# Transposing q on VectorE instead of TensorE in a fused attention and gated feed-forward kernel

## The chip, the cores and the metric

The kernel runs on one core of a Trainium2 chip. A core has five engines, each with its own instruction stream in order: TensorE (PE, matrix products; PEld in the profile is its weight load), VectorE (DVE), ScalarE (ACT), GpSimd (POOL) and SyncE (SP, which here only starts transfers). Sixteen DMA engines move data between the HBM and the on-chip SBUF. The metric is the device time of one execution in microseconds (us). The kernel before took 934.76 us, the median of three runs (934.28 to 935.01). The profiled execution took 934.53 us, and its instructions span 932.8 us; the TensorE clock was granted at 0.999 of full speed.

## The reference

```
kv  = einsum('bhsd,bhse->bhde', k, v)          # 8 x 8 x 576 x 64
out = einsum('bhsd,bhde->bhse', q, kv)
out = out / sqrt(mean(out*out, -1) + 1e-6) * g_norm
x   = out as (8*576, 8*64)                      # 4608 tokens of 512
h   = x @ w_in                                  # 512 -> 2048
g   = h * erf(softplus(h))
result = g @ w_out                              # 2048 -> 512
```

There is no softmax: each head multiplies q by the small 64 x 64 matrix k^T v, normalizes by the root of the mean square of its 64 outputs, and the 512 outputs of a token go through a gated feed-forward block. w_in and w_out arrive as 64-bit floats and are converted on the chip.

## The kernel before, in words

**Groups.** The 4608 tokens are worked in nine groups T of 512. Groups 0 to 7 are the first 512 rows of each of the eight batch entries; the remaining 64 rows of each entry are gathered in `x_last` and make group 8. The eight heads of a group are worked in four pairs p. So there are 32 pairs (T, p), and the pair after (T, p) is called `then` in the code.

**Attention of a pair.** TensorE needs q with the channels on partitions. For T = 0 the function `products` (L426) transposes q with TensorE; this stays. For the 28 pairs of T = 1 to 7, `turn_products` (L293) makes 16 products of 64 x 64 blocks of q with an identity matrix, and in every second pair 4 more for the last 64 rows (`q_last`); `turned` (L339) copies them from PSUM to the SBUF tile `qT` on ACT, and `tails_kept` (L352) copies the last rows on DVE. `kv_products` (L321) makes the 20 products of k^T v, and `kv_kept` (L361) stores the sum in `bd_kv`. `visit` (L459) multiplies qT by bd_kv into the PSUM tile `at`, ACT squares the result, and `mean` (L524) averages the squares over the channels of a head by a product with the matrix `mean_w`. `norm` (L558) finishes on DVE.

**Where turning and k^T v are done.** For T = 1 and 2 and for the pair (3, 0), `prepare` (L376) does turning and k^T v of a pair as a block of its own before the pair's visit (nine blocks). From T = 3 on (`fused`), the visit of a pair does both for the next pair, with the turned blocks in a pair of PSUM banks of their own (19 visits).

**Two kinds of mean.** In groups 2 to 7 (`halves`), `halve` (L517) splits the squares on DVE into a rounded upper part and a rest, both of type fp32r, and the mean is two products on these. In groups 0, 1 and 8 the mean is one plain fp32 product.

**Feed-forward.** Groups 0 and 1 run step by step (32 steps n, 16 to a group) with weights held in SBUF. While group 1 is worked the weights are cut into three parts each and stored to DRAM (`w_upper`, `w_lower`, L688 to L717). From group 2 on, h and the result are computed from such parts as sums of fp32r products (L677), in batches of four of the 16 column blocks; a batch is four products pairs for h and four for the result. The loop at L1014 runs over the 28 batches of groups 2 to 8. Each batch fetches the weight parts of the next one: four tiles w_in_parts and four w_out_parts of 768 KB each (`load_parts`, L807), from pools of 4 and 7 tiles. The attention of group T + 1 is cut into pieces and laid into the batches of group T, one pair to a batch; `places` (L1030) says after which product each piece comes. Everywhere the order of instructions is the order of the Python program, by hand (`manual_schedule`).

**Transfers.** Nearly all go out from SP, in program order. `load_pair` (L122) fetches q, k and v of a pair, two pairs ahead, into pools of two buffers. q of a pair is one transfer of 256 KB in runs of 256 bytes; k and v for T > 0 are each one transfer with 115 rows on the partition side and one of a single row; `load_last` (L147) fetches the last rows of q, four transfers to a group. In the compiled program SP's transfers use eight completion counters in turn, and each transfer waits for the one eight places before it to have landed.

Of the kernel before, what the change touches and what calls it, by code (L numbers as in the profile page):

```python
# [56 lines left out]
SHIFT = 4096.0  # L57


@with_exitstack  # L60
def kernel(
# [54 lines left out]
    q_last = const.tile([P, 2, 2, D], FP32, name="q_last")  # L116
# [5 lines left out]
    def load_pair(i):  # L122
        T, p = divmod(i, NP)
        if T >= B:
            return
        pool = early if i in (2, 3) else kvp
        side = nc.scalar if i < 3 else nc.sync
        t = q_sb[T, p] = pool.tile([P, J, 2, D], FP32, name="q_sb", tag="q")
        nc.sync.dma_start(
            out=t, in_=q[T, 2 * p : 2 * p + 2, 0:G, :].rearrange("h (p j) d -> p j h d", j=J)  # L130
        )
        for name, got, src in (("k", k_sb, k), ("v", v_sb, v)):
            C = chunks(T)
            rows, rest = divmod(S, C)
            assert rest < 2
            t = got[T, p] = pool.tile([rows + rest, 2, C, D], FP32, name=f"{name}_sb", tag=name)
            heads = src[T, 2 * p : 2 * p + 2]
            side.dma_start(
                out=t[:rows].rearrange("r h c d -> r h (c d)"),
                in_=heads[:, : S - rest].rearrange("h (r c) d -> r h (c d)", c=C),  # L140
            )
            if rest:
                side.dma_start(
                    out=t[rows:, :, 0], in_=heads[:, S - rest :].rearrange("h r d -> r h d")
                )

    def load_last(T, p):  # L147
        if T < B:
            nc.sync.dma_start(
                out=q_last[p % 2 * R : p % 2 * R + R, p // 2],  # L150
                in_=q[T, 2 * p : 2 * p + 2, G:S, :].rearrange("h r d -> r h d"),
            )
# [6 lines left out]
    for i in range(NP - 1):  # L159
        load_pair(i)  # L160
        if i == 0:
            load_last(0, 0)
            load_last(0, 1)
# [7 lines left out]
    ident = const.tile([P, P], FP32, name="ident")  # L171
    make_identity(nc, ident)
    mean_w = const.tile([P, P], FP32R, name="mean_w")
    mean_f = early.tile([P, P], FP32, name="mean_f", bufs=1)
# [118 lines left out]
    def turn_products(T, p, ps):  # L293


        qs = q_sb.pop((T, p))
        for j in range(J):
            for r in range(2):
                for i in range(2):
                    out_ = ps[r][rows_of[i if r == 0 else 1 - i], 0 : 2 * P]  # L300
                    yield partial(
                        nc.tensor.matmul,
                        out_.rearrange("d (t j) -> d j t", j=J)[:, j],
                        lhsT=qs[rows_of[r], j, i],
                        rhs=ident[rows_of[r], rows_of[r]],
                        start=True,
                        stop=True,
                    )
        if p % 2 == 0:
            for r in range(2):  # L310
                for i in range(2):
                    yield partial(
                        nc.tensor.matmul,
                        ps[r][rows_of[i], 2 * P : 2 * P + R],
                        lhsT=q_last[rows_of[r], p // 2, i],
                        rhs=ident[rows_of[r], rows_of[r]],
                        start=True,
                        stop=True,
                    )

    def kv_products(T, p, at, crossed):  # L321
# [4 lines left out]
        for c in range(C):  # L326
            for r in range(2):
                rows = (slice(0, D), slice(D, S // C + (c < S % C)))[r]
                for i in range(2):
                    yield partial(  # L330
                        nc.tensor.matmul,
                        at[rows_of[i], r ^ i if crossed else r, kv_cols],
# [5 lines left out]

    def turned(T, p, ps):  # L339

        qT = attp.tile([P, G], FP32, name="qT", tag="qT")
        if isinstance(ps, tuple):
            for a in range(2):
                nc.scalar.copy(halves_of(qT)[:, a], ps[a][:, 0 : 2 * P])
        else:
            nc.scalar.copy(halves_of(qT), ps[:, :, 0 : 2 * P])
        if p == NP - 2:
            for i in range(NP):
                load_last(T + 1, i)
        return qT  # L350

    def tails_kept(T, p, ps, qT):  # L352

        if p % 2 == 0:
            tails[T] = attp.tile([P, 2, R], FP32, name="qT_last", tag="t")
            for a in range(2):
                t = ps[a] if isinstance(ps, tuple) else ps[:, a]
                nc.vector.tensor_copy(out=tails[T][:, a], in_=t[:, 2 * P : 2 * P + R])
        ready[T, p] = qT, tails[T][:, p % 2]
# [16 lines left out]
    def prepare(T, p):  # L376

        at = at_tile()
        for product_ in turn_products(T, p, (at[:, 0], at[:, 1])):
            product_()  # L380
        for product_ in kv_products(T, p, at, crossed=False):
            product_()  # L382
        qT = turned(T, p, at)

        def keep():
            tails_kept(T, p, at, qT)
            kv_kept(T, p, at)

        kept.append(keep)
# [3 lines left out]
    def keep_prepared():  # L393
        kept.pop()()

    def attention(T, p, pools=None, in_parts=False):
# [3 lines left out]
        halves = FIRST <= T < B  # L400
        quad = 0 < T < B
        fused = FIRST < T < B
# [17 lines left out]
        def square_tile(name):  # L420
# [3 lines left out]
            return attp.tile([P, G], FP32, name=name, tag="sq_lo" if fused else "qT")  # L424

        def products():  # L426
# [17 lines left out]
            if p == NP - 2:  # L444
                for i in range(NP):
                    load_last(T + 1, i)
# [3 lines left out]
            if p % 2 == 0:  # L450
                tails[T] = attp.tile([P, P], FP32, name="qT_last", tag="t")
# [7 lines left out]
        def visit():  # L459


            qT, tail = ready.pop((T, p))
            at = st["at"] = at_tile()
            x = halves_of(qT)
            for a, i, o in ((0, 0, 0), (0, 1, 1), (1, 0, 1), (1, 1, 0)):
                nc.tensor.matmul(  # L466
                    at[rows_of[o], a, 0 : 2 * P],
                    lhsT=bd[rows_of[i], a * D : a * D + D],
# [4 lines left out]
            for s in rows_of:  # L473
                nc.tensor.matmul(
                    at[s, 0, 2 * P : 2 * P + R], lhsT=bd[s, 0:D], rhs=tail[s], start=True, stop=True
                )
            st["o"] = at[:, :, 0 : 2 * P]
            st["next"] = fused and then[0] < B
            if st["next"]:
                ps = pair_of_banks("q0_ps", "q1_ps")  # L480
                kvs = list(kv_products(*then, at, crossed=True))
                turns = list(turn_products(*then, ps))
                while kvs or turns:
                    for some in (turns, kvs):
                        for product_ in some[:4]:
                            product_()  # L486
                        del some[:4]
            if fused:
                st["sq"] = x_new.tile([P, G], FP32, name="sq", tag="x")
            else:  # L490
                st["sq"] = qT
            nc.scalar.activation(two(st["sq"]), st["o"], AF.Square)
            if st["next"]:
                st["turned"] = ps, turned(*then, ps)

        def keep_tail():
            nc.vector.tensor_copy(
                out=x_last[:, p, T * R : T * R + R], in_=st["at"][:, 0, 2 * P : 2 * P + R]
            )
            if st.get("next"):  # L500
                tails_kept(*then, *st.pop("turned"))
# [94 lines left out]
        if T == 0:  # L596
            return products, apply, halve, mean, norm
        if T == B:
            return lambda: None, square, lambda: None, mean, norm, split

        prepare_ = partial(prepare, T, p)
        if fused:
            first_ = (prepare_, keep_prepared) if (T, p) == (FIRST + 1, 0) else ()
            pieces = (first_, (visit, halve, keep_tail), (loads,))
        elif halves:
            pieces = ((prepare_,), (visit,), (halve, keep_tail, loads))
        else:
            pieces = ((prepare_, loads), (visit,), (keep_tail,))
        after = (split_upper, split_lower) if in_parts else (split,)
        return (*(partial(chain, *group) for group in pieces), mean, norm, *after)  # L610
# [163 lines left out]
    load_last(0, 2)  # L774
    load_last(0, 3)
# [11 lines left out]
    for i in range(NP + 3):  # L787
# [3 lines left out]
        if i == 1:  # L791
            for _ in range(RAW - 2):
                w_next("load")
            load_pair(NP)
            load_pair(NP + 1)
# [4 lines left out]
    w_late.append(True)  # L800
    first_batch, batches = FIRST * NB, NG * NB
# [17 lines left out]
    def pieces_of(T):  # L819


        steps = [([], [], []) for _ in range(FC)]
        for p in range(NP):
# [5 lines left out]
            steps[f + 2][0].append(halve)  # L829
# [34 lines left out]
    for n in range(FIRST * FC + 1):  # L864
# [10 lines left out]
        if T < FIRST:  # L875
# [5 lines left out]
            while kept:  # L881
                keep_prepared()
            for key in list(w_new)[:2]:
# [37 lines left out]
        if T < FIRST:  # L921
# [21 lines left out]
            if n == 0:  # L943
                w_next("split")
            for piece in steps[f][1]:
# [68 lines left out]
    for m in range(first_batch, batches + 1):  # L1014
        T, b = divmod(m, NB)
        todo = []
        turn = b == NB - 1 and T + 1 < B
        if T + 1 < NG:
            todo = list(attention(T + 1, b, in_parts=turn))
# [11 lines left out]
        if T + 1 == B:  # L1031
            places = (0, 0, 0, 5, 6, 7)
            if b == NB - 1:


                places, todo[3] = (0, 0, 0, 4, 6, 7), partial(todo[3], table=False)
                todo[5] = partial(chain, todo[5], softplus_table)
        elif turn:


            places, todo[3] = (0, 2, 3, 4, 5, 5, 6), partial(todo[3], table=False)
# [10 lines left out]
        to_last = m == B * NB - 1  # L1052
# [33 lines left out]
        if m < batches:  # L1086
            for i in range(1 if turn else 2):
# [5 lines left out]
        for j in range(J):  # L1093
# [12 lines left out]
            else:  # L1106
                due_halves = range(2) if j == (2 if to_last or turn else 1) else ()
            if to_last or turn:
                pieces(BATCH + 1 + j)
            if turn and j == 0:  # L1110
# [43 lines left out]
```

## Time and profile before

| | us | what it is |
|---|---|---|
| run, median of 3 | 934.76 | 934.28 to 935.01 |
| span of the profiled execution | 932.8 | first to last instruction |
| PE busy | 916.4 | 98% of the span, 5998 products |
| DVE busy | 728.5 | 78% |
| ACT busy | 603.4 | 65% |
| products of the turning in visits (L486, q_ps) | 20.6 and 3.1 | 608 on q_sb, 72 on q_last |
| products of the turning in blocks (L380) | 6.3 and 1.5 | 288 on q_sb, 40 on q_last |
| ACT copies of turned q (L344, L346) | 12.1 and 5.3 | 38 of 128x256, 9 of 128x512 |

Busy time of a group of instructions is the time in which at least one of them ran; products are pipelined and several 64 x 64 products run at once, so these times overlap with each other and with other rows. An fp32 product shows as two records. What a block of products costs is better read from the times at which it and the next block start.

### The profile page before, as it was taken

The numbers are of one execution on the slowest core, as the hardware profiler recorded it, in microseconds if no ns is written. First come the engines' busy times: TensorE is split into PE (matmuls) and PEld (weight loads), VectorE is DVE, ScalarE is ACT, GpSimd is POOL, SyncE is SP. The second block draws the span as 40 slices with busy tenths as digits, with TensorE's granted clock in tenths as the row PEclk, the third lists the DMA queues.
The fourth block names the chain that finished last, engine by engine and source line by source line (L and its number), as shares of the span: only waits on it lengthen the run. The fifth ranks groups of instructions, "written<-read, shape, count | busy, mean of one in ns | idle before, by whom it ended". The sixth has DMA issues, their size and how long they took to land.

```text
span 932.8 us, 15394 instructions
## 1 busy us (share of the span) xinstructions
PE 916.4 (98%) x5998; PEld 684.5 (73%) x5998; DVE 728.5 (78%) x1074; ACT 603.4 (65%) x830; POOL 2.4 (0%) x10
## 2 busy tenths in 40 slices
PE   6999999999999999999999999999999999999998
PEld 4444445665588888888888888888888888888886
DVE  2888848888578888888878888888888887886777
ACT  3877666777666666666656666666666766665552
POOL 1000000000000000000000000000000000000000
PEclk9999999999999999999999999999999999999999
DMA  9866406888799998899889989988897778778871
GB/s 257 288 207 211 144 1 224 312 344 316 225 352 320 334 332 283 293 338 316 286 295 321 317 297 308 324 311 299 282 345 269 270 265 333 286 282 312 330 270 53
DMA packets 108272, 260.01 MB, mean 279 GB/s; under 512 B 43992, under 2 KB 66856, under 8 KB 108200
## 3 DMA queue, kind: packets, MB, share of 16 engines
q1 hardware_dynamic: 106488, 256.73, 78.2%
q10 hardware_dynamic: 1648, 2.29, 0.8%
q8 instruction: 48, 0.79, 0.3%
q14 instruction: 24, 0.20, 0.1%
q0 software_dynamic: 64, 0.00, 0.0%
HBM read 224.40 MB, written 34.60 MB: 278 GB/s over the span
## 4 chain that ended last, share of the span: by engine, by line
PE 94%; ACT 2%; DVE 2%; DMA 1%; issue 0%; DVEq 0%; ACTq 0%
PE n_ps L677 47%; PE m_ps L677 23%; PE o_ps L733 9%; PE h_ps L914 6%; PE at_ps L466 2%; PE at_ps L486 1%; PE q_ps L486 1%; PE at_ps L380 1%; PE at_ps L537 1%; PE at_ps L538 1%; PE ms_ps L543 1%; PE at_ps L382 1%; DMA v_sb<-in_v_dram 1%; DMA q_sb<-in_q_dram 1%; DVE w_new L645 0%
## 5 line engine op out<-in xcount | busy, mean ns | idle before, releaser
L677 PE MATMUL n_ps<-w_out_parts,g_forms 128*128 128x512 f32 x928 | 231.9, 392 | 0.0
L677 PE MATMUL n_ps<-x_forms,w_in_parts 128*128 128x512 f32 x896 | 224.2, 392 | 0.0
L677 PEld LDWEIGHTS n_ps<-w_out_parts,g_forms 128*128 128x128 f32 x928 | 172.8, 188 | 37.2 <-issue 1.9
L677 PEld LDWEIGHTS n_ps<-x_forms,w_in_parts 128*128 128x128 f32 x896 | 166.5, 188 | 35.3
L1082 ACT ACTIVATE s<-h 128x512 f32<-128x512 f32 x112 | 70.8, 632 | 176.1 <-DVE h L655 176.0
L655 DVE TENSOR_TENSOR h<-m_ps,h 128x512 f32<-128x512 f32 x116 | 80.0, 689 | 80.6 <-ACT h L1067 55.7
L677 PE MATMUL m_ps<-w_out_parts,g_forms 128*128 128x512 f32 (+1 forms) x468 | 124.3, 388 | 0.0
L677 PE MATMUL m_ps<-x_forms,w_in_parts 128*128 128x512 f32 x448 | 119.8, 389 | 0.0
L733 PE MATMUL o_ps<-w_out_sb,h_sb 128*128 128x512 f32 x224 | 101.7, 597 | 0.2 <-DVE h_sb L862 0.2
L677 PEld LDWEIGHTS m_ps<-w_out_parts,g_forms 128*128 128x128 f32 x468 | 87.4, 188 | 18.5
L677 PEld LDWEIGHTS m_ps<-x_forms,w_in_parts 128*128 128x128 f32 x448 | 84.1, 188 | 17.6
L655 DVE TENSOR_TENSOR e<-m_ps,e 128x512 f32<-128x512 f32 (+1 forms) x117 | 80.4, 687 | 14.8 <-PE m_ps L677 3.6
L1067 ACT ACTIVATE h<-n_ps 128x512 f32<-128x512 f32 x112 | 66.1, 591 | 19.0 <-PE n_ps L677 18.9
L733 PEld LDWEIGHTS o_ps<-w_out_sb,h_sb 128*128 128x128 f32 x224 | 41.4, 189 | 44.6 <-issue 41.9
L621 DVE SCALAR_TENSOR_TENSOR g_forms<-g_forms 128x1024 fp32r<-128x1024 f32 x58 | 71.1, 1225 | 2.0
L618 DVE TENSOR_TENSOR g_forms<-h,g_forms 128x1024 fp32r<-128x1024 f32 x58 | 70.6, 1217 | 0.1
L615 ACT ACTIVATE g_forms<-h 128x1024 fp32r<-128x1024 f32 x58 | 58.4, 1050 | 15.1 <-PE m_ps L677 11.1
L1114 DVE TENSOR_TENSOR h<-h,s 128x1024 f32<-128x1024 f32 x56 | 65.9, 1218 | 0.0
L914 PE MATMUL h_ps<-xT,w_in_sb 128*128 128x512 f32 x144 | 64.8, 596 | 0.2 <-DVE w_in_sb L245 0.2
L650 DVE SCALAR_TENSOR_TENSOR e<-n_ps,e 128x512 f32<-128x512 f32 x88 | 60.2, 684 | 3.9 <-PE n_ps L677 3.9
L108 ACT ACT_TABLE_LOAD x44 | 56.5, 1283 | 0.7
L1088 ACT ACTIVATE s<-s 128x1024 f32<-128x1024 f32 x51 | 51.5, 1054 | 0.3
(129 smaller groups left out, 1028.9 us busy)
## 6 DMA issues: line engine op xcount, KB each, us to landing
w_out_parts<-w_out SPq DMA_DIRECT2D x116, 768.0 KB
w_in_parts<-w_in SPq DMA_DIRECT2D x112, 768.0 KB
w_in<-w_new SPq DMA_DIRECT2D x16, 768.0 KB
q_sb<-in_q_dram SPq DMA_DIRECT2D x32, 256.0 KB
w_raw<-in_moe_w_in_dram SPq DMA_DIRECT2D x16, 512.0 KB
w_raw<-in_moe_w_out_dram SPq DMA_DIRECT2D x8, 1024.0 KB
out_dram<-e SPq DMA_DIRECT2D x32, 256.0 KB
k_sb<-in_k_dram SPq DMA_DIRECT2D x28, 287.5 KB
```

The lines of the kernel that those rows point to most:

```text
L108: nc.scalar.preload_act_table_set("softplus")
L615: nc.scalar.activation(high, x, AF.Copy, scale=1.0 + 2.0**-13)
L618: nc.vector.tensor_tensor(out=low, in0=x, in1=high.bitcast(FP32), op=ALU.subtract)
L621: nc.vector.scalar_tensor_tensor(out=both, in0=low.bitcast(FP32), scalar=SHIFT, in1=high.bitcast(FP32), op0=ALU.mult, op1=ALU.add,)
L650: nc.vector.scalar_tensor_tensor(out=out_, in0=ps, scalar=scale, in1=out_, op0=ALU.mult, op1=ALU.add)
L655: nc.vector.tensor_tensor(out=out_, in0=ps, in1=out_, op=ALU.add)
L677: nc.tensor.matmul(ps[:, cols], lhsT=weights(form, k), rhs=moving(form, k)[:, cols], start=(form == forms[0] and k == 0), stop=(form == fo ...
L733: nc.tensor.matmul(o_ps[j], lhsT=g[:, j * P : j * P + P], rhs=w_out_sb[:, f, :], start=(f == 0), stop=last,)
L914: nc.tensor.matmul(plain[i], lhsT=w_in_sb[:, i % FC, c], rhs=xT[T][:, c, :], start=(c == 0), stop=(c == KC - 1),)
L1067: nc.scalar.activation(h[:, i], n_ps, AF.Copy, scale=SHIFT - 1.0)
L1082: nc.scalar.activation(s[:, i], h[:, i], AF.Softplus)
L1114: nc.vector.tensor_tensor(out=part(h, half), in0=part(h, half), in1=part(s, half), op=ALU.mult)
```

## The change

For T = 1 to 7 q is no longer turned by TensorE.

- `load_q` fetches q of a pair (all 576 rows, last rows included) in eight transfers of 32 partitions, in runs of 32 floats (128 bytes), so that each 32 x 32 block of the tile is a block of q. `turn` transposes the tile in 32 x 32 blocks by one DVE instruction on 128 x 576 elements. It is called once per pair: at the end of `norm` of the pair before (T = 1, 2), or after the loads of the pair before (T > 2, place 3 of its batch). `turn_products`, `turned` and `tails_kept` go, and `load_last` remains for T = 0 alone.
- In `load_pair` q now comes after k and v. The first two pairs of group 1 are fetched later, after group 0's attention.
- k^T v of the next pair joins the visit for all T from 1 on; only the pair (1, 0) still has a block of its own. The visit no longer takes a pair of PSUM banks.
- Halves of the squares, and so fp32r means, are made in three more pairs of group 1 (not the first) and in the four of group 8. In groups 1 and 2 `halve` and what follows the visit on DVE run before the cutting of weights of the same step.
- In the last batch of group 7 the pieces of group 8 are placed like those of other groups; group 8's pieces come at places 0, 0, 2, 5, 7, 8.
- `q_last`, `ident` and `mean_f` move to other pools; tiles named qT grow to 576 columns.

```diff
+    def load_q(i):
+        T, p = divmod(i, NP)
+        t = q_sb[T, p] = kvp.tile([P, S], FP32, name="q_sb", tag="q")
+        for n in range(P // SQ):
+            h, w = divmod(n, D // SQ)
+            to = t[n * SQ : n * SQ + SQ].rearrange("a (j b) -> a j b", b=SQ)
+            for head, js in ((1 - h, slice(0, G // 2 // SQ)), (h, slice(G // 2 // SQ, S // SQ))):
+                src = q[T, 2 * p + head, :, w * SQ : w * SQ + SQ]
+                nc.sync.dma_start(
+                    out=to[:, js], in_=src.rearrange("(j a) b -> a j b", a=SQ)[:, js]
+                )
...
-    def turn_products(T, p, ps):
...
+    def turn(T, p):
+        if T < B:
+            qT = ready[T, p] = qt_tile("qT")
+            nc.vector.transpose(out=qT, in_=q_sb.pop((T, p)))
...
-        for product_ in turn_products(T, p, (at[:, 0], at[:, 1])):
-            product_()
         for product_ in kv_products(T, p, at, crossed=False):
             product_()
-        qT = turned(T, p, at)
...
-        halves = FIRST <= T < B
+        halves = T > 1 or (T == 1 and p > 0)
...
-            st["next"] = fused and then[0] < B
-            if st["next"]:
-                ps = pair_of_banks("q0_ps", "q1_ps")
-                kvs = list(kv_products(*then, at, crossed=True))
-                turns = list(turn_products(*then, ps))
...
+            if then[0] < B:
+                for product_ in kv_products(*then, at, crossed=True):
+                    product_()
...
-        prepare_ = partial(prepare, T, p)
-        if fused:
-            first_ = (prepare_, keep_prepared) if (T, p) == (FIRST + 1, 0) else ()
-            pieces = (first_, (visit, halve, keep_tail), (loads,))
-        elif halves:
-            pieces = ((prepare_,), (visit,), (halve, keep_tail, loads))
-        else:
-            pieces = ((prepare_, loads), (visit,), (keep_tail,))
+        first_ = (partial(prepare, T, p),) if (T, p) == (1, 0) else ()
+        then_ = partial(turn, *then)
+        if apart:
+            pieces = (first_, (visit, halve, keep_tail), (loads, then_))
+            return (*(partial(chain, *group) for group in pieces), mean, norm, *after)
+        pieces = (first_, (visit, loads), (halve, keep_tail) if halves else (keep_tail,))
+        return (*(partial(chain, *group) for group in pieces), mean, partial(chain, norm, then_), *after)
...
-            load_pair(NP)
-            load_pair(NP + 1)
+            load_pair(NP, turned=False)
+            load_pair(NP + 1, turned=False)
...
     w_late.append(True)
+    load_q(NP)
...
-            steps[f + 2][0].append(halve)
+            steps[f + 2][3].append(halve)
...
             while kept:
                 keep_prepared()
+            for piece in steps[f][3]:
+                piece()
             for key in list(w_new)[:2]:
                 w_lower(*key)
...
-            places = (0, 0, 0, 5, 6, 7)
...
+            places = (0, 0, 2, 5, 7, 8)
```

## The prediction

> **What bounds the kernel now.** I read the page's busy shares and chain first, then the products by form, then the timeline of TensorE at one place of each kind, and last SP's timeline and the DMA share by stretch.
>
> ```profile
> PE 916.4 (98%) x5998; PEld 684.5 (73%) x5998; DVE 728.5 (78%) x1074; ACT 603.4 (65%) x830; POOL 2.4 (0%) x10
> PE 94%; ACT 2%; DVE 2%; DMA 1%; issue 0%; DVEq 0%; ACTq 0%
> ```
>
> TensorE is busy for all but 16 us, and 94% of the chain that ended last is TensorE. Most of the gaps lie in the first 28 us; so a product taken off TensorE shortens the run by its own pace, unless something else falls behind.
>
> The timeline (start, length, product; an fp32 product is two records) shows that pace. First a block before the visit of (1, 0), then one without last rows, then a visit from T = 3 on:
>
> ```profile
> 41.88 0.69 PE L380 MATMUL at_ps<-ident,q_sb 64*64 64x64 f32 x32
> 42.39 0.30 PE L380 MATMUL at_ps<-ident,q_last 64*64 64x64 f32 x8
> 42.51 0.76 PE L382 MATMUL at_ps<-v_sb,k_sb 64*64 64x64 f32 x40
> 43.20 3.70 PE L914 MATMUL h_ps<-xT,w_in_sb 128*128 128x512 f32 x8
> ...
> 75.25 1.03 PE L543 MATMUL at_ps<-qT,mean_w 128*128 128x256 f32 x4
> 76.11 1.02 PE L733 MATMUL o_ps<-w_out_sb,h_sb 128*128 128x512 f32 x2
> ...
> 170.25 0.69 PE L380 MATMUL at_ps<-ident,q_sb 64*64 64x64 f32 x32
> 170.76 0.76 PE L382 MATMUL at_ps<-v_sb,k_sb 64*64 64x64 f32 x40
> ...
> 259.58 0.66 PE L466 MATMUL at_ps<-qT,bd_kv 64*64 64x256 f32 x8
> ```
>
> Turning costs 0.51 us a pair, 0.12 more with last rows; k^T v 0.69; a plain mean 0.86.
>
> The second resource near its limit is the transfers. SP's issues in one batch, the DMA share of two stretches, and that of T = 3 to 7 (second figure from the end of a row):
>
> ```profile
> 427.20 3.04 SPq L815 DMA_DIRECT2D w_in_parts<-w_in  x2
> 430.30 0.67 SPq L129 DMA_DIRECT2D q_sb<-in_q_dram  x1
> 431.02 0.58 SPq L138 DMA_DIRECT2D k_sb<-in_k_dram  x1
> ...
> 438.24 0.32 SPq L815 DMA_DIRECT2D w_out_parts<-w_out  x1
> ...
> 419.00:423.00 4.00, 4.00 (x20) 3.30 (x19) 3.86 (x6) 3.91 (x5) 0.00 (x0) 1.00 1.03 430
> 411.00:413.00 2.00, 2.00 (x11) 1.65 (x10) 1.70 (x6) 0.34 (x2) 0.00 (x0) 1.00 0.36 109
> ...
> 255.00:744.00 489.00, 489.00 (x3697) 401.95 (x3696) 402.96 (x600) 320.18 (x443) 0.00 (x0) 1.00 0.89 308
> ```
>
> Weights alone flow at 430 GB/s with all DMA engines busy; while k and v flow, a third of them work. The mean is 0.89. TensorE waits for no weights, but there is little room.
>
> [...] No row of this trace shows a VectorE transpose. [...] share 0.36 of 16 is 5.7 engines while k and v flow. [...] The trace's DMA records agree in kind: 18 ns for 256 bytes, 46 for 1024.
>
> **The change part by part, in T = 1 to 8.**
>
> Turning, TensorE. Nine pairs had a block: 9 x 0.51 + 5 x 0.12 = 5.2 us. Nineteen were turned inside a visit. The block that starts at 259.58 lasts 1.75 us to the next h product, the one at 283.84, with last rows, 1.86. Left of it stay 0.49 for the eight visit records, 0.11 for the tail's, and 0.69 for k^T v: 1.29. So 10 x 0.46 + 9 x 0.57 = 9.7 us. Together 14.9 us, all on the path.
>
> Means. The code makes seven means one-pass: (1,1) to (1,3) and four of group 8. Four fp32r records take 0.47 us (269.62 to 270.09 in the timeline), a plain mean 0.86; group 8's have as many columns. 7 x 0.39 = 2.7 us. Their halving adds 7 x (0.43 + 0.69) = 7.8 us to DVE.
>
> Order in T = 2. The mean waited 0.5 and 0.8 us (L537) because halving stood behind the cutting of weights on DVE; it now stands ahead. I take half, 0.7 us; bounds 0 and 1.4.
>
> DVE. [...] 28 x 0.78 = 21.8, less 28 tail copies of 0.22 each (4.9 us by the rows), plus 7.8: 728.5 becomes 753 us of some 915, 82%. In a batch, 19.8 of 24 us busy becomes 20.4 of 23.8[...]. The transposed tile is used a batch later, and what is queued behind the transpose (the add that frees m_ps) has two more pairs of banks to wait on. I cost it at nothing. ACT loses 17.4 us of copies, hidden anyway.
>
> SP and DMA. Per pair one issue of 0.67 becomes eight of about 0.64 (that of q_last's similar transfers): 4.5 us more, and four q_last issues per group go. The 1024 packets of 256 bytes and 128 for the last rows become 2304 of 128. From 18 ns for 256 and 46 for 1024 I get 13.6 ns by a straight line; bounds 9 (a 4-byte packet) and 37 (the pitch of 256-byte packets in a crowded batch). I take 14: 144 packets per engine, 2.0 us instead of 1.3.
>
> The waits matter more. A transfer waits for the one eight places before. Behind k, its row, v, its row come eight q pieces: the fifth now waits for k, the seventh for v. Before, only one q stood here, and the weights were issued while k and v were moving. Now the next weights are issued after v has landed: 1.1 us after its last packet (L815 at 438.24 follows k's last packet, at 437.1, by that), two pieces of 0.64, and 0.95 to the first packet (L815 at 846.5, first packet at 847.47). The five busy engines then need per batch: eight tiles at 430 GB/s 14.6, k and v 5.4 (589 KB at 109 GB/s), and 3.4 idle or on q; 23.4 us. A batch takes 24.3 now and 23.8 after. One batch in four also stores 1 MB of results, 2.4 us. A group: 4 x 23.4 + 2.4 = 96.0 against 95.2. Five groups lack 0.8 each, 4 us; the first of them starts with a lead of 2.5 us (last w_out tile landed at 264.4 by its packets, used at 266.9). So 1.5 us comes back as waits for weights, and I add 1 us in T = 1 and 2, where the stores of cut weights stand behind the pieces. Sum 2.5; bounds 0 and, at 37 ns, some 40.
>
> Sum: 932.8 - 14.9 - 2.7 - 0.7 + 2.5 = 917.0 us of span. The median run is 2.0 above the profiled span: **919 us**, 917.5 to 924 in this case. Chance 0.35.
>
> **Rivals.** *The queue stays hidden.* Issues of 0.5 instead of 0.64, or k and v in 5.0 instead of 5.4, bring the batch's need below 23.2, and the sum is 914.5 to 917.5. For it: leads of the last tile of a batch by packets are 4 to 9 us in the steady part. Chance 0.33.
>
> *The queue takes half back.* If each weight tile takes 2% longer, or landing takes 1.5 us, the need is 24; 20 batches lose 0.3 to 0.6 each: 924 to 933. Slow transposes would end here too, by way of T = 2, where DVE is busy 89.5 of 115 us. Chance 0.18.
>
> *Slower than before: small packets decide.* [...] Price: 144 ns a batch for each nanosecond per packet. When the pieces' own data fills the time, need is 14.6 + 5.4 + 0.6 + 144 t; 20 batches lose the 18.3 us won when it exceeds 24.7, at t = 28 ns. At 37 ns it is 25.9, and the run about 958. Against it: 18 ns is what the records show for packets twice as long. Chance 0.10, with 0.04 left for a greater gain than 914 through shorter waits elsewhere.
>
> **How the numbers follow.** About 0.2% (1.9 us) is what a measurement of this kernel tells from no change. The first two cases and two thirds of the third lie within 914 to 930, 0.80. Faster: 0.35 + 0.33 + 0.18 + 0.04 less 0.02 for a loss just as large as the gain: 0.88; same 0.03; slower 0.09.
>
> **What would show it.** Rows L486 q_ps, L380 and L344 gone; 28 DVE transposes, about 0.8 us each; 5998 records down to about 4990; a visit block near 1.3 us; DVE near 82%. If the queue binds, waits of PE for DMA w_out_parts or w_in_parts appear after 266 us, and SP's list shows it waiting for v_sb and q_sb. The prediction is wrong if a 128-byte packet takes 25 ns or more, or if the q tile lands late and DVE waits for it, holding all behind it.

## The result and the profile after

The changed kernel takes 929.04 us (median of 4 runs, 928.31 to 929.87), against 934.53 for the kernel before (4 runs beside it); the ratio is 0.9941, with a 95% interval of 0.9924 to 0.9958. So it is faster by 5.5 us, where 15.8 were forecast: the time lies in the range, but the gain is a third of the forecast. The case written down for 924 to 933 us, with a chance of 0.18, is the one that came.

The page of the changed kernel, busy shares and the chain that ended last:

```profile
PE 898.8 (97%) x4990; PEld 668.6 (72%) x4990; DVE 751.0 (81%) x1088; ACT 589.9 (64%) x783; POOL 2.4 (0%) x10
PE 76%; DMA 11%; DVE 6%; ACT 5%; issue 1%; SPq 1%; DVEq 0%; ACTq 0%
```

TensorE does 17.6 us less work (916.4 before), which is what was forecast for turning and means (14.9 + 2.7). That it fits to the tenth is luck: the means alone, in before_means below, show 2.3. But the span fell by 6.3 us only (932.8 to 926.5). The chain says where to look: before, 94% of it was TensorE; now a quarter is transfers, VectorE and ACT. The waits of TensorE name them (who waited, for whom: us in total, times, longest):

```profile
PE n_ps L634 <- ACT h_sb L889: 3.4, 1, 3.4
PE n_ps L634 <- ACT h L889: 2.8, 1, 2.8
PE n_ps L634 <- DMA w_in_parts<-w_in: 2.1, 2, 1.7
PE at_ps L435 <- DVE qT L318: 2.0, 1, 2.0
PE n_ps L634 <- DMA w_out_parts<-w_out: 1.7, 2, 0.9
...
PE n_ps L634 <- ACT h L1024: 0.8, 1, 0.8
PE n_ps L634 <- ACT sq L454: 0.3, 1, 0.3
```

None of these seven stood in the profile before. They are 13.1 us in three places: 6.2 in T = 2 (the two copies of h by ACT), 2.0 in T = 1 (the first turned q), and 4.9 in T = 3 to 7 (3.8 for weights, 1.1 behind ACT). The two waits of a mean in T = 2 (0.8 and 0.5) are gone. So 17.6 + 1.3 - 13.1 = 5.8 of the 6.3.

**T = 2.** The first of the two waits in the timeline: SP (seven of the eight pieces; the view starts behind the first), then ACT, then TensorE (start, length, engine and line).

```profile
177.88 6.83 SPq L162 DMA_DIRECT2D q_sb<-in_q_dram  x7
188.13 0.63 ACT L596 ACTIVATE w_new<-w_out_sb 128x512 fp32r<-128x512 f32 x1 [1.44 <-DMA w_out<-w_new]
190.12 0.63 ACT L596 ACTIVATE w_new<-w_in_sb 128x512 fp32r<-128x512 f32 x1 [1.36 <-DMA w_in<-w_new]
190.66 0.62 ACT L902 ACTIVATE s_sb<-h_sb 128x512 f32<-128x512 f32 x1
191.29 1.28 ACT L911 ACT_TABLE_LOAD   x1
192.59 2.19 ACT L911 ACTIVATE s_sb<-s_sb 128x512 f32<-128x512 f32 x4
194.78 1.28 ACT L109 ACT_TABLE_LOAD   x1
196.08 0.63 ACT L572 ACTIVATE x_forms<-x 128x512 fp32r<-128x512 f32 x1
196.61 0.58 ACT L889 ACTIVATE h_sb<-n_ps 128x512 f32<-128x512 f32 x1
190.22 3.60 PE L690 MATMUL o_ps<-w_out_sb,h_sb 128*128 128x512 f32 x8
197.25 0.49 PE L634 MATMUL n_ps<-x_high,w_new 128*128 128x512 f32 x1 [3.42 <-ACT h_sb L889]
```

SP spends 6.8 us on these seven pieces, and the stores of cut weights stand behind them. ACT can't cut the next weights until those stores have emptied the w_new buffers. Its two waits for them, 1.44 and 1.36 us, make it 2.8 us late at the end of the batch, where table loads, erf and the cutting of x follow one another without a pause, ahead of the copy that frees n_ps. At the same place before, the copy and TensorE's work were

```profile
195.93 0.58 ACT L929 ACTIVATE h_sb<-n_ps 128x512 f32<-128x512 f32 x1
194.68 3.60 PE L733 MATMUL o_ps<-w_out_sb,h_sb 128*128 128x512 f32 x8
198.21 0.69 PE L380 MATMUL at_ps<-ident,q_sb 64*64 64x64 f32 x32
198.84 0.78 PE L382 MATMUL at_ps<-v_sb,k_sb 64*64 64x64 f32 x40
199.56 0.50 PE L677 MATMUL n_ps<-x_high,w_new 128*128 128x512 f32 x1
```

The copy was done 3.1 us before n_ps was needed: TensorE came to its o_ps products 4.5 us later than it does now, and the old block of turning and k^T v (1.35 us) stood between the o_ps and the n_ps products. The change moved its k^T v behind n_ps, into the visit.

**T = 1.** From the chain around 48 us: the last piece of q (1, 0) is held until a load of expert weights has landed.

```profile
36.09 9.79 DMA w_raw<-in_moe_w_out_dram
...
45.90 1.74 DMA q_sb<-in_q_dram
...
47.72 0.79 DVE qT L318
...
48.65 0.66 PE at_ps L435 x8
```

**T = 3 to 7.** DMA share and GB/s are the last two figures of a row of the windows; first two stretches of the changed kernel in the batch at 400 us, then the same two of the kernel before:

```profile
412.00:416.00 4.00, 4.00 (x21) 3.34 (x20) 3.86 (x5) 3.95 (x5) 0.00 (x0) 1.00 0.56 188
416.00:420.00 4.00, 4.00 (x19) 3.33 (x18) 3.77 (x6) 3.91 (x5) 0.00 (x0) 1.00 0.41 99
```

```profile
412.00:416.00 4.00, 4.00 (x21) 3.38 (x20) 2.75 (x5) 2.41 (x4) 0.00 (x0) 1.00 0.82 240
416.00:420.00 4.00, 4.00 (x20) 3.28 (x20) 3.79 (x6) 3.96 (x5) 0.00 (x0) 1.00 1.03 334
```

Before, weights flowed while k and v did. Now nothing but k, v and the pieces is on its way for some microseconds: in the DMA records of T = 3 to 7 the 6144-byte packets of the weights pause once a batch, for 6.3 us on average (18 pauses of more than 3 us, 113 us in all; before, 2 such pauses, and 19 of more than 1 us, 35 us in all).

The sizes of these waits are those of one execution. Other kernels below that leave the transfers of T = 2 as they are (q_early, dve2, spread3) show 3.6 to 4.4 us there in place of 6.2, with the granted clock of TensorE halved for 3 to 7 us behind the gap, and two of them 1.0 and 6.4 us of waits for weights in place of 3.8. So each size is good to some 2 us.

### The profile page after: what moved, and what is told of

Same layout as the page of the kernel before. It is cut to its first block, busy times and chain, and to the rows that moved or that the text cites. A ratio compares the mean times of both kernels' runs of the same rounds, so it can differ in the third digit from the quotient of the medians.

```text
span 926.5 us, 13591 instructions
## 1 busy us (share of the span) xinstructions
PE 898.8 (97%) x4990; PEld 668.6 (72%) x4990; DVE 751.0 (81%) x1088; ACT 589.9 (64%) x783; POOL 2.4 (0%) x10
## 4 chain that ended last, share of the span: by engine, by line
PE 76%; DMA 11%; DVE 6%; ACT 5%; issue 1%; SPq 1%; DVEq 0%; ACTq 0%
PE n_ps L634 41%; PE m_ps L634 20%; PE o_ps L690 6%; PE h_ps L874 4%; DMA w_out_parts<-w_out 4%; DMA w_in_parts<-w_in 2%; DMA w_in<-w_new 2%; DMA v_sb<-in_v_dram 1%; PE at_ps L449 1%; PE at_ps L435 1%; DMA w_raw<-in_moe_w_out_dram 1%; ACT s_sb L911 1%; DMA q_sb<-in_q_dram 1%; DVE h L612 1%; PE at_ps L496 1%
## 5 line engine op out<-in xcount | busy, mean ns | idle before, releaser
L634 PEld LDWEIGHTS m_ps<-x_forms,w_in_parts 128*128 128x128 f32 x448 | 84.1, 188 | 17.6
L874 PEld LDWEIGHTS h_ps<-xT,w_in_sb 128*128 128x128 f32 x144 | 27.1, 190 | 33.4 <-issue 31.6
```

What stands on the lines that cost most here:

```text
L634: nc.tensor.matmul(ps[:, cols], lhsT=weights(form, k), rhs=moving(form, k)[:, cols], start=(form == forms[0] and k == 0), stop=(form == fo ...
L874: nc.tensor.matmul(plain[i], lhsT=w_in_sb[:, i % FC, c], rhs=xT[T][:, c, :], start=(c == 0), stop=(c == KC - 1),)
```

## The experiments

Each kernel ran beside the kernel before, whose median was 934.5 to 935.0 us each time. The two questions of the first four: is it the pieces, and is it VectorE?

**q_two: the pieces taken away.** This kernel leaves out the rearranging of q, so it prices the transfers and is no use as a kernel.

```diff
-        for n in range(P // SQ): ... (eight pieces)
+        nc.sync.dma_start(out=rows, in_=...)          # 512 columns, as before the change
+        nc.sync.dma_start(out=t[:, G:S], in_=...)     # the last 64
```

> The changed kernel, but each pair's q from T = 1 on comes in two transfers from SP (one as before the change, one for the last 64 columns) instead of eight pieces. The values of q that are used are therefore wrong; everything that is computed, its shapes and the order on the engines are those of the changed kernel. Theory 'SP's issues': the three kinds of new gaps on TensorE (3.4 + 2.8 us in T = 2 behind ACT's copies of h, 4.8 us of waits for weights in T = 3 to 7, 2.0 us for the first turned q) all go, and the run takes 929.0 - 13 = 916 us (914 to 918). Rival 'VectorE': the gaps in T = 2 come from what was added to VectorE (28 turns, the halving); then the 6.2 us stay, and the run is 921 to 924.

Measured: 920.67 us, 8.4 less than the changed kernel. No wait for weights is left, nor the one in T = 1; in T = 2 there remain

```profile
PE n_ps L631 <- ACT h_sb L886: 1.9, 1, 1.9
PE n_ps L631 <- ACT h L886: 1.0, 1, 1.0
```

that is 2.9 of 6.2. The time lies between the two forecasts (914 to 918 and 921 to 924): the pieces cost most of the 13 us, but 2.9 us in T = 2 stay without them. New waits of 2.7 us for the means that stand in the last batch of a group take a part of the gain back.

**dve2: every turn done twice.**

```diff
+            for _ in range(2):
                 nc.vector.transpose(out=qT, in_=q_sb[T, p])
```

> The changed kernel with every turn of q done twice on VectorE, 28 x 0.77 = 21.5 us more of VectorE. Theory: a turn has room on VectorE, which is 81% busy; the run takes 929 to 932 us. Rival 'VectorE': the loss comes from VectorE being full in T = 2, where it is 90 of 115 us busy; four more turns there lengthen the two gaps by their own length each, and the visits elsewhere wait as well: 935 us or more.

Measured: 930.64 us. 28 more turns add 18.8 us of VectorE (769.8 against 751.0) and 1.6 us of time, as forecast. VectorE isn't what the time is lost to. Its room is not large, though: in this profile TensorE waits 5.0 us in all for means in T = 3 to 7 that VectorE brings late, and for weights 1.0 in place of 3.8.

**q_pool and q_first: the pieces at another place.**

```diff
-                nc.sync.dma_start(          # q_pool
+                nc.gpsimd.dma_start(
```

```diff
+        if T > 0 and turned:               # q_first: ahead of the loop over k and v
+            load_q(i)
         for name, got, src in (("k", k_sb, k), ("v", v_sb, v)):
```

> The changed kernel with the eight q pieces of a pair issued by GpSimd's queue instead of SP's; same pieces, same packets. Theory 'SP's issues': it is SP's time and its places in the rotation that cost, not the packets of 128 bytes; the run takes 916 to 919 us, with no wait of ACT for stores of cut weights over 2.5 us in T = 2. Rival 'packets': the small packets hold up the weights and the stores on the DMA engines; then at least 8 of the 13 us stay and the run is 924 to 929. If issuing from GpSimd is slow itself (no row shows its price), VectorE waits for DMA q_sb.

> The changed kernel with the eight q pieces ahead of the pair's k and v on SP instead of behind them. They then don't wait for k and v to land, but take as many issues. Theory 'SP's issues', part window: half of the time that SP spends on the pieces is waiting for k and v; weights in T = 3 to 7 are issued sooner, 4.8 us of waits fall to 0 to 1.5, and the two gaps in T = 2 (6.2 us) shrink to 2 to 5; the run takes 921 to 925 us. Rival 'issues alone': only the number of issues counts, and the run stays at 927 to 929.

Measured: q_pool 936.91 us and q_first 948.61, both worse than leaving the pieces where they are, against either expectation for q_first and worse than the rival's for q_pool. In q_first the pieces follow the weights directly, and SP's part of the waits (whole run) and one batch read

```profile
SPq L161 <- DMA w_in_parts<-w_in: 83.4, 59, 2.4
...
SPq L161 <- DMA w_out_parts<-w_out: 35.1, 32, 1.5
...
417.97 13.47 SPq L161 DMA_DIRECT2D q_sb<-in_q_dram  x8
```

Each piece now waits for a weight tile eight places before it, so eight pieces take 13.5 us instead of 5 to 8, and k, v and the next weights are issued after that. I had asked what the pieces wait for where they stood, and not what they would wait for at the new place. In q_pool SP had no pieces to issue, and weights, k, v and pieces flowed at the same time; yet TensorE waited 13.6 us for weights. k and v of a pair took 14.7 us from first to last packet, where they take 5.4 in the changed kernel (medians, T = 3 to 7), and SP waited 84 us for them with the weights. So SP's time alone isn't it either. The kernel wasn't quite what I had expected: GpSimd's pieces stand in the DMA records as 128 packets a pair of 2048 or 2560 bytes, not as 2304 of 128, so it changes the packets too, and says nothing of small ones.

**kv128: k and v in 128 rows.** The third suspect: k and v, in 115 rows, keep few DMA engines busy. Where no other packets are in flight in T = 3 to 7, their 1280-byte packets stand five at a time in the DMA records for 13.6 of 19.1 us in the changed kernel (4.8 of 6.6 before), and six for most of the rest; the 6144-byte packets of the weight tiles, which have 128 rows, stand sixteen at a time for 206 of 282 us (159 of 255 before). So k and v are said here to be on five of sixteen engines. That 128 rows spread k and v as they do the weights is the author's estimate from these counts, and is not shown for kv128.

```diff
+                t = got[T, p] = pool.tile([P, 2, C, D], FP32, name=f"{name}_sb", tag=name)
+                side.dma_start(out=t[:, :, 0:J]..., in_=heads[:, 0:G] as (r c) rows, c=4)   # 128 rows
+                side.dma_start(out=t[0:R, :, J], in_=heads[:, G:S]...)                      # 64 rows
```

> The changed kernel with k and v of a pair (T = 1 to 8) fetched as 128 rows of four and 64 rows of one, instead of 115 rows of five and one row more: as many transfers[...]. k^T v has 36 records a pair instead of 40, 112 x 18 ns = 2.0 us less on TensorE. Theory: a piece of q costs little by itself; what costs is that it waits for k or v, eight places before it, which take 5.4 us on five engines. Then the waits for weights in T = 3 to 7 (4.8 us) go, the gaps in T = 2 shrink by the 3.2 us that they shrank by with q in two transfers, and the run takes 929 - 2.0 - 4.8 - 3.2 = 919 us (917 to 922). Rival 'issues alone': eight issues of 0.6 us on SP cost the same wherever k and v go; the run takes 925 to 928.

Measured: 919.48 us with the same eight pieces as the changed kernel. The theory's 919 is met, in part by luck: the 2.0 us of products didn't come (see the next run), the wait of 2.0 in T = 1 went, which the sum didn't have, and 2.9 us of waits for means came. But its two main terms came as forecast: no wait of TensorE for weights is left, and the gaps in T = 2 fell from 6.2 to 3.1. SP's pieces hardly wait for v any more; in T = 3 to 7 the line is 26.8 us in the changed kernel and 1.8 here:

```profile
SPq L162 <- DMA v_sb<-in_v_dram: 26.8, 18, 1.7
```

```profile
SPq L173 <- DMA v_sb<-in_v_dram: 1.8, 4, 0.9
```

The pieces wait about as long as before, but for weights (w_in_parts 40.0 us against 23.1). The pause in the weights fell from 6.3 to 4.4 us a batch. Two readings fit. One is the theory's: a wait of the pieces for v leaves most engines empty (DMA share 0.41 at 416 to 420 us, above), one for weights doesn't. The other is that five engines carry k and v on top of their share of all else, and set the pace of the weights. This run changes both at once and doesn't tell them apart; spread3, below, where the pauses are gone and the time is worse, speaks for the second.

**before_kv128: the same rows in the kernel before.**

> The kernel before with the same new rows of k and v (128 of four, 64 of one). Theory: there the transfers of k and v are hidden, so only the 2.0 us of products go: 933 us (932 to 934). Rival: k and v on five engines cost time before the change too, and the run falls below 931.

Measured: 934.54 us beside 934.96, ratio 0.9997 (0.9989 to 1.0005): nothing. k and v on five engines were hidden before, so the rival falls; they cost time only together with the pieces. The 2.0 us of products didn't come: a block of k^T v of its own takes 0.68 us with 36 records, where it took 0.69 to 0.71 with 40, and a visit's takes 0.78 in kv128 against 0.79 in the changed kernel (medians of 28). Why the four fewer records save nothing is not shown; of the two halves of the rows, one still has its five chunks. So in kv128 nearly all of the gain is from the transfers.

**q_eight: number or packets?** q_two with eight transfers.

```diff
+        nc.sync.dma_start(out=rows, in_=...)                       # 512 columns
+        for n in range(7):                                         # the last 64
+            nc.sync.dma_start(out=t[a : a + SQ, ...], in_=...)
```

> q_two with eight transfers a pair instead of two, at the same place in SP's order: the first 512 columns in one, as before the change, the last 64 in seven small ones (736 packets a pair where q_two has 640 and the changed kernel 2304). The values of q that are used are again wrong. It separates the number of transfers from the number of packets. Theory 'SP's issues' (an issue takes 0.6 us, and each waits for the transfer eight places before): the run is near the changed kernel, 926 to 930 us. Rival 'packets': it is near q_two, 920 to 923.

Measured: 925.70 us, between the two: 5.0 us more than q_two for six more transfers, 3.3 less than the changed kernel for 1568 fewer packets a pair. It is just below the range of the first theory and above that of the rival. Number and size both seem to count, though the eight transfers here are one large and seven small, so they also differ in what stands behind what.

**visit_early and visit_only: the rest of T = 2.**

```diff
-            steps[f + 1][1].append(apply)
+            steps[f + 1][3 if T == FIRST else 1].append(apply)
```

> The changed kernel with the visit of a pair of T = 2 (its products with k^T v and the next pair's k^T v, 1.3 us of TensorE) issued before the n_ps products of its step instead of after them, as the old block of turning and k^T v stood. Theory: in q_two 3.0 us of gaps stayed in T = 2, since ACT's chain at the end of a batch (softplus, table, erf, table, cutting x, copy of h) is what n_ps waits for, and before the change 1.35 us of products stood in front of that wait. Then the two gaps shrink by 1.3 us each and the run takes 926.4 us (925.5 to 927.5). Rival: the place makes no difference because the visit itself waits for something as late; the run stays at 929.

> visit_early again, with the loads of k, v and q left at their old place in the step, so that only the visit of T = 2 moves ahead of the n_ps products. In visit_early the loads had moved with it, and ACT waited up to 8.4 us for stores of cut weights behind them. Theory: 2 x 1.3 us of work now stands in front of the wait for ACT's copy of h; the run takes 926.4 us (925.5 to 928). Rival: the visit's own operands or bank are as late; 929.

visit_only has, besides, a line that issues `load_pair` at its old place.

Measured: visit_early 932.76 us, visit_only 926.25. In visit_early the loads had moved with the visit, ahead of the stores, and ACT waited longer than ever:

```profile
184.42 0.63 ACT L596 ACTIVATE w_new<-w_out_sb 128x512 fp32r<-128x512 f32 x1 [8.39 <-DMA w_out<-w_new]
```

With the loads left in place, the gaps in T = 2 fell from 6.2 to 2.9 us, and the run by 2.8, as forecast. But the profile doesn't bear out that the one is the cause of the other. Behind the gap that is left, the granted clock is 0.50 from 197.4 to 204.2, and the products that follow are slow. The first and the end of the same twelve records in visit_only, and in the changed kernel the end (its start, 197.25, is shown above):

```profile
198.20 0.80 PE L635 MATMUL n_ps<-x_high,w_new 128*128 128x512 f32 x1 [2.85 <-ACT h_sb L892]
...
203.49 0.97 PE L691 MATMUL o_ps<-w_out_sb,h_sb 128*128 128x512 f32 x1
```

```profile
200.19 0.66 PE L435 MATMUL at_ps<-qT,bd_kv 64*64 64x256 f32 x8
```

They take 5.3 us, against 2.9. Of the 3.3 us of smaller gaps at least 2.3 are lost again: the batches after T = 2 (first n_ps product on w_in_parts) start at 250.7 us, 251.4 in the changed kernel and 253.9 before. The rest of the gain comes later, where this edit changes nothing: waits for weights are 1.6 us in place of 3.8. So what the work ahead of the wait is worth is not shown.

**kv128_visit.** Both edits.

> kv128 with the visit of T = 2 ahead of the n_ps products, loads at their old place. In kv128 two gaps of 1.1 and 2.0 us were left in T = 2, and 1.3 us of visit can stand in each. Theory: 919.5 - 1.1 - 1.3 = 917 us (916.5 to 918). Rival: the gaps move to the next wait; 919.5.

Measured: 919.82 us, no better than kv128, as the rival had it; the gaps in T = 2 fell from 3.1 to 2.3 us only. In the profile the batches after T = 2 start 1.5 us earlier than in kv128 (244.4 against 245.9), and later stages take it back, waits of means 1.0 of it.

**q_early: the first turned q.**

```diff
+        if i == 3:
+            load_q(NP)
...
-    load_q(NP)
```

> The changed kernel with the eight pieces of q of (1, 0) issued after the third round of expert weights in the attention of T = 0, where SP stands still for 4 us, instead of behind the last load. In the changed kernel the last of them waits for a load of weights to land at 45.9 us, VectorE's first turn starts at 47.7 and the visit of (1, 0) waits 2.0 us. Theory: that wait goes and nothing else changes: 927 us (926.5 to 928). Rival: the loads of weights that now stand behind the pieces come later and h products wait instead; 929 or more.

Measured: 928.41 us (926.04 to 929.53), between theory and rival. The wait of 2.0 us is gone, and it stays gone through T = 2: the batches start at 249.2 us, 2.2 earlier than in the changed kernel. (The gaps in T = 2 are smaller, 3.6 us, but behind the larger one the granted clock, third figure from the end, is half for over 6 us.)

```profile
194.00:200.00 6.00, 4.98 (x12) 3.81 (x12) 5.18 (x8) 4.27 (x8) 0.00 (x0) 0.50 0.92 375
```

The 2.2 us go in T = 3 to 7, where TensorE waits 6.4 us for weights in place of 3.8. A lead won ahead of a stage that waits for transfers can be spent waiting there.

**before_means: the means alone.**

```diff
-        halves = FIRST <= T < B
+        halves = T > 1 or (T == 1 and p > 0)
```

> The kernel before with that part of the change alone that makes seven plain means one-pass (pairs 1 to 3 of T = 1, four of the group of last rows), with their halving on VectorE. Theory: 7 x 0.39 us of TensorE less, nothing else: 934.9 - 2.7 = 932.2 us (931.5 to 933). Rival: halving comes late on VectorE and TensorE waits for it, as two means of T = 2 do; no gain, 934 to 936.

Measured: 934.26 us, ratio 0.9994 (0.9987 to 1.0002). TensorE's work fell by 2.3 us (916.4 to 914.1), but halving delayed two other things on VectorE:

```profile
PE h_ps L914 <- DVE w_in_sb L245: 1.4, 1, 1.4
...
PE n_ps L677 <- DVE x_forms L618: 0.8, 1, 0.8
```

The rival's forecast was right, though not by waits of the means. These waits aren't in the changed kernel, where halving and the last group's pieces stand at other places, so this run doesn't price the means there; it shows that the part alone gains nothing.

**spread3, spread2, kv128_spread: place or amount?** What was open after these: do the pieces cost because eight stand in a row, or because the engines have no room?

```diff
-                nc.sync.dma_start(
+                waiting.append(partial(nc.sync.dma_start, ...))
...
                 w_now.setdefault(key, []).append(t)
+            some_q(2)          # two pieces behind each weight tile
```

In spread3 the pairs loaded up to T = 2 keep their eight pieces in a row; in spread2 those loaded in T = 2 are spread too, by a `some_q(1)` behind the stores.

> The changed kernel with the q pieces of the loads in T = 3 to 7 issued two at a time behind each of the next four weight tiles instead of eight in a row behind v. Same pieces, packets and number of issues; k and v still on five engines. Theory 'place': the weights are issued while k and v move, and the 4.8 us of waits for weights fall to 0 to 1: 924 to 925.5 us, the gaps in T = 2 (6.2) and T = 1 (2.0) as in the changed kernel. Rival 'amount': the DMA engines have no room for k, v and the pieces, wherever the pieces stand; 927.5 to 930.

> spread3 with the same for the loads in T = 2: one piece at a time behind the stores of cut weights. Theory 'place': ACT's waits for those stores shrink and the two gaps in T = 2 fall from 6.2 to about the 3.0 us that q_two left, so 921 to 923 us. Rival 'amount': no better than spread3, or worse since more stores now stand behind a piece.

> kv128[...] with the pieces of spread2. Theory: in kv128 no wait for weights was left, so spreading can win only in T = 2, where two gaps of 3.1 us in all are ACT's own chain: 919 us (917.5 to 920.5), about the same as kv128. If it is below 917, the pieces in a row still cost something in kv128.

Measured: 939.17, 934.00 and 917.22 us. With k and v in 115 rows spreading is worse than the row of eight, far above the theory's forecasts, and for spread3 above the rival's too; with k and v in 128 rows it is better, just below its forecast of 917.5 to 920.5. Of T = 3 to 7 in spread3, waits and the stretch as a whole:

```profile
PE n_ps L644 <- DMA w_in_parts<-w_in: 7.5, 6, 2.5
PE n_ps L644 <- DMA w_out_parts<-w_out: 4.6, 5, 1.2
```

```profile
255.00:744.00 489.00, 476.40 (x2984) 383.84 (x2983) 408.09 (x590) 305.31 (x400) 0.00 (x0) 1.00 0.94 307
```

The same stretch of the changed kernel has a DMA share of 0.83 and 311 GB/s. In T = 2 spread2 did what was expected (its two gaps are 2.9 us), but in T = 3 to 7 it lost as much as spread3 (12.5 us of waits for weights). So the engines are busier and move less: the pauses are gone, and weights are on their way all the time, but k and v of a pair take 8.5 us from first to last packet where they took 5.4 (medians of the 1280-byte packets in T = 3 to 7), and pieces and weights stand waiting for them (pieces 38.5 us for k, weights 30.4 for v). The packets themselves are slower: their median is 74 and 76 ns in spread3 and spread2, and 55 in the other kernels with 115 rows. In the kernels with k and v in 128 rows no wait for weights remains in either order. kv128_spread gains on kv128 in T = 2, where it has one gap of 1.1 us instead of two of 3.1 in all, with the visit still behind the n_ps products; its batches after T = 2 start at 243.5 us, 2.4 earlier than in kv128. It is the fastest kernel here: ratio 0.9807 (0.9793 to 0.9822) to the kernel before, 11.8 us below the changed kernel.

## Why the prediction was wrong

- **Turning and means on TensorE, -14.9 and -2.7: right.** Busy time fell by 17.6 us (2.3 for the means by before_means), and the rows for turned q are gone, with 4990 records as forecast.
- **VectorE, 753 us and 82%: right** (751.0, 81%). A turn takes 0.77 us for 128 x 576 fp32 (768 to 779 ns). The forecast's 0.78 was the author's estimate; no row of the kernel before showed a VectorE transpose. dve2 shows that there was room for as many turns again at a cost of 1.6 us.
- **Order in T = 2, -0.7: both waits of means went**, 1.3 us, within the bounds.
- **"The transposed tile is used a batch later ... I cost it at nothing": wrong by 2.0 us.** The first one, (1, 0), isn't fetched a batch ahead; its last piece waits for a load of weights. The rule of eight places was in the prediction, but not applied to this place.
- **"I add 1 us in T = 1 and 2, where the stores of cut weights stand behind the pieces": this is the term that was most mis-sized. The place and the mechanism were right, the size was 6.2 us in T = 2.** ACT stood 5.0 us idle for these stores in the two batches (1.44 and 1.36 shown above, 2.15 at the second), and came that much later to the copy that TensorE waits for, but for 1.3 us that it then waited for n_ps in the second. The 1 us was put without working out how long ACT would wait for the stores, or what slack it had. Nor did the sum have the cover: TensorE now comes earlier to the wait, and the block of k^T v that stood in front of it, at most 1.3 us a wait, stands behind. How the 6.2 divides stays open. q_two takes 3.3 of it away, kv128_spread 5.1 with the visit left behind n_ps, and visit_only narrows the gaps by 3.3 but gains little of that by the end of T = 2.
- **"1.5 us comes back as waits for weights": 3.8, and 1.1 behind ACT.** The mechanism fits: k, v and pieces alone on the way, weights issued after the pieces that wait for v. The number of busy engines is as the forecast had it (five 1280-byte packets at a time, under kv128), and in kv128, with 128 and 64 rows in place of 115, these waits are gone. The packets were priced well (median 13 ns for 128 bytes, 14 taken; that they spread evenly, 144 to an engine, was the author's estimate), and k and v too (5.4 us, 5.4 taken). But the forecast of this wait rested on the difference of two numbers near 23 us a batch, and each tenth there is 2 us over 20 batches.
- **The terms that were mis-sized are the returns:** 2.5 us in the sum (1.5 + 1), 13.1 measured. 8.2 of the 13.1 came in T = 1 and 2, where 1 had been put. The case "the queue takes half back" had the right total, but by another way: waits for weights in T = 3 to 7, or slow transposes. That its range came is luck. The rival of small packets as such (28 ns and more) fell.

Open: whether the pieces cost by their waits for v or by the load on five engines; and why pieces mixed with weights slow k and v on five engines as they do in spread3, q_pool and spread2. That they do is measured; how an engine shares its time between transfers no run here shows. A kernel with pieces that stand behind v but wait for nothing there, k and v on five engines, would tell the first.

## What to carry to other kernels

When work is taken off the bounding engine, list what the other engines have ready at each place where it stood, with the slack: an engine that comes 4 us earlier meets waits that it never saw, and a block that is moved takes its cover along. Follow each new transfer to what stands behind it in its issuer's order, and from there to the engine that waits. Before one transfer is made into eight, see what each of them will wait for in its issuer's rotation, and which engines are empty meanwhile; a transfer on a third of the engines that was hidden can become the bound then, and giving it another number of rows may be worth more than the change itself (9.6 us in kv128, 0.4 in the kernel before, which is within its noise). And a wait that has gone from a list is no gain yet: in visit_only most of it went into slow products, in q_early into other waits. Compare the times at which the same product starts at the end of each stage.

## What the runs showed of the hardware

- The granted clock of TensorE fell to half beside some gaps. It was 0.50 for 6.8 us in q_early, q_first, spread3 and visit_only, and for 10.2 in visit_early, beside gaps of 2.9 to 6.8 us in T = 2, and for 3.4 us in q_two, q_eight and dve2, beside gaps of 1.9 to 3.1; in the changed kernel's profile a gap of 3.4 us passed with the clock at 1.00. So the length of a gap alone didn't decide it; what did is not shown. Products of 512 columns that start 0.23 us apart in the changed kernel start 0.43 apart in such a stretch of visit_only, so 6.8 us at half the clock can cost, as an estimate from these two, 3.2 us on top of the gap.
- GpSimd's issue of a piece took 0.60 us of its own time in q_pool (some 133 us in the run), SP's 0.45 us in the changed kernel (medians).
- A VectorE transpose of 128 x 576 fp32 values in 32 x 32 blocks took 768 to 779 ns in the changed kernel, and from 767 in q_pool.
- SP's transfers signal eight semaphores in turn in the traces before and after, so a transfer has the semaphore of the one eight places before, and waits for it: of the eight pieces the fifth for k, the seventh for v. In T = 3 to 7 of the changed kernel the pieces waited 10.1 us for k and 26.8 for v.
- The median packet took 9 ns for 4 bytes, 13 for 128, 18 for 256, 46 for 1024, 55 for 1280 and 234 for 6144 in the changed kernel.
- Products of 64 x 64 overlapped: the 608 that turned q in visits of the kernel before took 134 us in sum (median 218 ns) and kept TensorE busy for 20.6.
